# The last spread of O on VectorE instead of GpSimd, with the projection's change of layout ahead of K of pair 31, in a decode-layer kernel

## Chip, cores and metric

The kernel runs on one core of one Trainium2 chip. The metric is the device time of one execution in microseconds (us), and medians over several executions are given. The profile adds a "span", which starts with the first instruction and is in most executions about 1.2 us shorter than the device time. The "granted clock" is the share of TensorE's full clock that the profile shows as granted, 1 or a half in these traces.

## The reference

One decode step of a layer, batch 2, one new token each, D = 512, 32 heads of 128, a KV cache of 8192 positions, then a gated feed-forward of 1376:

```python
q = heads(layernorm(x) @ wq)                                # 32 heads of 128
p = softmax(einsum("bhqd,bhkd->bhqk", q, k_cache) * 128**-0.5)
h = x + merge_heads(einsum("bhqk,bhkd->bhqd", p, v_cache)) @ wo
y = layernorm(h)
gate, up = y @ W_gate, y @ W_up
out = h + ((gate * (gate > 0)) * up) @ W_down
```

The caches are 4 MB for each pair of heads and each of K and V; 281 MB are read in all. That reading sets the time.

## The kernel before

The 64 (batch, head) rows are handled as 32 "pairs" of heads (numbered 0 to 31), two pairs to a round. For each pair the loads bring a 4 MB tile of K and one of V ("K30", "V31" and so on). VectorE computes the scores of three quarters of the positions, of half of them for pair 31 (one multiply, four halving adds, one reduce), TensorE those of the rest (transposes, evacuation by ScalarE, matmuls). ScalarE takes exps, and TensorE multiplies by V ("PV"). After each round the four outputs O are normalised (those of a round while the next one runs) on VectorE and "spread": copied into a sparse matrix `O_l` and a selector `rsel`, from which a small matmul (the "gather") collects the O of all heads but the last two. That spread was GpSimd's:

```python
def o_spread(g):
    pool.wait(t_oc[g], tok("og", g))
    if g >= 1:
        p0, p1 = first(2 * g - 2)[0], first(2 * g - 1)[0]
        pool.run(nc.gpsimd.memset(O_l[:, :, :, p0:min(p1 + NM, 128)], 0.0))
        pool.last()
    for a in range(2):
        p0, off = first(2 * g + a)
        n = min(NM, 128 - p0)
        nc.gpsimd.tensor_copy(out=rsel[:, a, :], in_=rows[:, DR - off:2 * DR - off])
        i = nc.gpsimd.tensor_tensor(out=O_l[:, a, :, p0:p0 + n],
                                    in0=..., in1=..., op=ALU.mult)      # O_cur times mask, cut
    i.then_inc(l2p, 1)
```

TensorE's tail, after the loop over the rounds (P0 = pair 30, P1 = pair 31):

```python
k_part(tail, P0, 1, ...)          # transposes and scores of K30
o_gather(tail)                    # waits for the spread
for r in range(DR): ...           # projection of 30 of the 32 heads by wo: 30 matmuls of 512
k_part(tail, P1, 8, ...)          # transposes and scores of K31, 8 groups
for c in range(DC): ...           # "W": brings the projection into the layout of h
pv(tail, P0, ...)                 # PV30
nc.tensor.wait_ge(a2p, 19)        # all exps of 31
z_sum(tail, Sp[0])                # sums of exps
pv(tail, P1, ...)                 # PV31: first half of V31, then the second
```

Then follow the last two heads' projection, the residual, and the feed-forward: W_up (44 matmuls), W_gate (44), W_down (4 on a piece loaded early, then 40 on three blocks), and the output. The loads of W_up, W_gate and the three W_down blocks are issued in this order after VectorE's multiply of K30 has freed the slot.

The softmax here doesn't subtract the row's maximum and nothing guards it: scores larger than these inputs give would overflow.

## Time and profile before

| | before |
|---|---|
| device time, median | 663.15 us (662.45 to 663.22) |
| span of the profiled execution | 661.4 us |
| HBM read | 281 MB, 425 GB/s over the span |
| share of 16 DMA engines' time with packets | 99.1% |

In all views PE is TensorE, PEld its weight loads, DVE VectorE, ACT ScalarE, POOL GpSimd, and SPq the queue of SyncE, which issues the loads.

DMA is busy to the last slice (9 tenths in 39 of the 40 slices, 6 in the last), so no work in the tail can bring the end far forward: it must wait for the last bytes.

The timeline of GpSimd in the kernel before, around the last two spreads: start in us from the span's start, duration, engine, line, operation, tiles, shape.

```profile
594.08 0.21 POOL L490 COPY rsel<-rows 128x30 bf16<-128x30 bf16 x1
594.24 0.21 POOL L491 TENSOR_TENSOR O_l<-O_cur,mask 128x12 bf16<-128x12 bf16 x1
...
619.01 6.46 POOL L490 COPY rsel<-rows 128x30 bf16<-128x30 bf16 x1
625.42 0.21 POOL L491 TENSOR_TENSOR O_l<-O_cur,mask 128x12 bf16<-128x12 bf16 x1
625.57 3.33 POOL L490 COPY rsel<-rows 128x30 bf16<-128x30 bf16 x1
628.86 0.21 POOL L491 TENSOR_TENSOR O_l<-O_cur,mask 128x10 bf16<-128x10 bf16 x1
```

VectorE in the same stretch of the kernel before:

```profile
618.57 0.16 DVE L470 TENSOR_TENSOR O_cur<-Ob,zi 128x4 bf16<-128x4 f32 x1
618.84 6.56 DVE L516 TENSOR_TENSOR prod<-slot,q_b 128x12288 bf16<-128x12288 bf16 x1
625.43 6.83 DVE L522 TENSOR_TENSOR prod<-prod 128x6144 bf16<-128x6144 bf16 x4
```

The same copy takes 0.21 us in one round and 6.46 us in the last. In the last round VectorE runs its multiply of K30 from 618.84 to 625.40 and its first halving add from 625.43 to 628.84, and the two copies end when these end, at 625.47 and 628.90. The other 28 copies of this form (L490) in the trace ran while VectorE had no instruction, and took 0.207 to 0.209 us each. What in the two VectorE instructions holds up the copies is not shown.

The chain of waits of the kernel before, its end: start, duration, what.

```profile
619.01 6.46 POOL rsel L490
...
625.63 3.28 POOL rsel L490
...
629.75 3.58 PE O L421 x30
633.32 1.03 PE T L349 x4
...
648.30 1.86 PE O L367 x32
...
653.41 1.70 PE S L659 x44
...
655.46 1.66 PE O L659 x44
...
657.55 1.37 PE O L711 x44
```

The spread holds up the projection (L421), that holds up K31's transposes (L349), and so on to PV31 (L367), W_up and W_gate (L659), W_down (L711). No load stands in this last stretch. From the trace's DMA records I took when the last of a transfer's 16 completions landed: V31's second half 647.1, W_up 650.4, W_gate 653.7, last W_down block 656.9. Compute is behind these by only 0.6 to 3 us, so that is what there is to win.

### The profile page before, as it was taken

Reading aid. Unit: us, or ns where it says so; the run is one execution under the profiler, and the core shown is the slowest. Engines: PE = TensorE matmul, PEld = TensorE weight load, DVE = VectorE, ACT = ScalarE, POOL = GpSimd, SP = SyncE. Lnnn points to the kernel's source line nnn. Section 1 sums busy time; section 2 is a strip of 40 time slices with the busy share of each in tenths; the row PEclk is TensorE's granted clock in tenths of the full one; section 3 lists DMA queues with packets and bytes.
Section 4 is the critical chain, followed back from the end, with each engine's and each line's share of the span. In section 5 each row is a group of like instructions: output and inputs, shape, how many; then the busy total and the mean of one; then the engine's idle time right before and its main releaser. Section 6 shows DMA issues by size and latency. Waiting matters only on the chain.

```text
span 661.4 us, 7674 instructions
## 1 busy us (share of the span) xinstructions
PE 333.3 (50%) x3220; PEld 203.4 (31%) x3220; DVE 465.0 (70%) x277; ACT 198.6 (30%) x418; POOL 34.0 (5%) x126
## 2 busy tenths in 40 slices
PE   2652354444555444645535364554536444454487
PEld 2431322223333122423313243232324322232254
DVE  1775576788767678776767877676886767687681
ACT  0531331233332223333223333322323322232360
POOL 2000000000000000000000000000000000000510
PEclk9995565556555656565555565655565565555787
DMA  9999999999999999999999999999999999999996
GB/s 381 430 415 428 444 421 432 436 422 442 426 432 438 425 432 432 428 440 426 432 434 424 440 427 430 438 428 434 432 427 434 430 432 432 430 437 430 426 424 257
DMA packets 10787, 281.23 MB, mean 425 GB/s; under 512 B 1202, under 2 KB 1556, under 8 KB 1940
## 3 DMA queue, kind: packets, MB, share of 16 engines
q1 hardware_dynamic: 10760, 281.06, 99.1%
q8 instruction: 6, 0.10, 0.1%
q14 instruction: 9, 0.07, 0.0%
q10 hardware_dynamic: 12, 0.00, 0.0%
HBM read 281.05 MB, written 0.00 MB: 425 GB/s over the span
## 4 chain that ended last, share of the span: by engine, by line
DMA 76%; DVE 16%; PE 4%; POOL 2%; ACT 1%; issue 0%; SPq 0%; DVEq 0%
DMA slot<-in_A_k_cache_dram 76%; DVE prod L516 15%; POOL rsel L490 1%; PE O L367 1%; DVE prod L522 1%; ACT kT L547 1%; PE O L421 1%; PE T L349 0%; PE Ob L377 0%; PE W L428 0%; PE S L659 0%; PE O L659 0%; PE S L337 0%; PE O L711 0%; DVE scores L527 0%
## 5 line engine op out<-in xcount | busy, mean ns | idle before, releaser
L516 DVE TENSOR_TENSOR prod<-slot,q_b 128x12288 bf16<-128x12288 bf16 (+1 forms) x32 | 207.7, 6491 | 152.5 <-DMA slot<-in_A_k_cache_dram 150.7
L522 DVE TENSOR_TENSOR prod<-prod 128x6144 bf16<-128x6144 bf16 (+4 forms) x128 | 210.3, 1643 | 4.4
L367 PE MATMUL O<-slot,e 128*16 128x512 bf16 x1024 | 118.5, 616 | 185.3 <-ACT e L454 129.7
L547 ACT ACTIVATE kT<-T 128x1024 bf16<-128x1024 bf16 x132 | 131.0, 1022 | 189.3 <-PE T L349 186.0
L349 PE MATMUL T<-ident_f,slot 128*128 128x128 f32 x528 | 121.8, 390 | 51.6 <-POOLq L534 51.6
L349 PEld LDWEIGHTS T<-ident_f,slot 128*128 128x128 f32 x528 | 87.9, 200 | 66.8 <-issue 66.7
L367 PEld LDWEIGHTS O<-slot,e 128*16 128x16 bf16 x1024 | 25.9, 112 | 251.8 <-ACT e L454 157.6
L454 ACT ACTIVATE e<-scores 64x96 bf16<-64x96 f32 (+1 forms) x64 | 19.4, 303 | 209.9 <-DVE scores L527 209.4
L337 PE MATMUL S<-q2c,kT 128*128 128x4 bf16 x1056 | 49.8, 169 | 39.0 <-ACT kT L547 38.7
L337 PEld LDWEIGHTS S<-q2c,kT 128*128 128x128 bf16 x1056 | 42.7, 106 | 67.3 <-ACT kT L547 65.3
L377 PE MATMUL Ob<-sel,os_sb 128*128 128x4 f32 x136 | 30.2, 345 | 24.9 <-ACT os_sb L562 24.2
L377 PEld LDWEIGHTS Ob<-sel,os_sb 128*128 128x128 f32 x136 | 28.7, 312 | 26.8 <-ACT os_sb L562 25.6
L527 DVE TENSOR_REDUCE scores<-prod 128x96 f32<-128x768 bf16 (+1 forms) x32 | 30.2, 945 | 1.1
L499 POOL COPY q2c<-q 128x8 bf16<-128x8 bf16 x32 | 9.1, 284 | 235.1 <-DMA slot<-in_A_v_cache_dram 221.2
L485 POOL MEMSET O_l<- 128x40 bf16 (+1 forms) x14 | 1.9, 136 | 325.9 <-DVE O_cur L470 325.9
L490 POOL COPY rsel<-rows 128x30 bf16<-128x30 bf16 x30 | 15.6, 520 | 34.4 <-DVE O_cur L470 33.5
L454 ACT ACTIVATE e<-S 64x32 bf16<-64x32 f32 (+1 forms) x64 | 13.0, 203 | 14.4 <-PE S L337 14.0
L454 ACT ACTIVATION_READ_ACCUMULATOR e<-S 64x1 f32 x64 | 12.8, 201 | 0.7
L454 ACT ACTIVATION_READ_ACCUMULATOR e<-scores 64x1 f32 x64 | 11.8, 184 | 0.0
L383 PEld LDWEIGHTS Ob<-zs,ones_f 128*128 128x128 f32 x30 | 7.0, 292 | 12.8 <-issue 12.8
L562 ACT ACTIVATE os_sb<-O 128x512 f32<-128x512 f32 x16 | 9.6, 597 | 3.2 <-PE O L367 2.8
L298 ACT ACTIVATE q_b<-O 128x512 bf16<-128x512 f32 x8 | 4.3, 595 | 17.4 <-PE O L293 17.4
(90 smaller groups left out, 85.6 us busy)
## 6 DMA issues: line engine op xcount, KB each, us to landing
slot<-in_A_k_cache_dram SPq DMA_DIRECT2D x32, 4096.0 KB, 32.3
slot<-in_A_v_cache_dram SPq DMA_DIRECT2D x31, 4096.0 KB, 30.6
slot<-in_A_wq_dram SPq DMA_DIRECT2D x1, 4096.0 KB, 12.3
slot<-in_A_v_cache_dram SPq DMA_DIRECT2D x2, 2048.0 KB, 28.0
X<-in_A_wo_dram SPq DMA_DIRECT2D x1, 3840.0 KB, 46.5
slot<-in_B_W_up_dram SPq DMA_DIRECT2D x1, 1376.0 KB, 25.0
slot<-in_B_W_gate_dram SPq DMA_DIRECT2D x1, 1376.0 KB, 27.9
slot<-in_B_W_down_dram SPq DMA_DIRECT2D x2, 512.0 KB, 29.1
```

Source lines behind the costliest of these rows:

```text
L337: i = nc.tensor.matmul(Sp[p % 2][:, 2 * jj:2 * jj + 4], lhsT=kv_[:, k, r, :], rhs=q2c[p % 2][:, r, :], start=(r == 0), stop=(r == 1))
L349: i = nc.tensor.transpose(Tp[g % 2][:, k * 128:(k + 1) * 128], k_t[:, j:j + 2, :].rearrange("p j d -> p (j d)").bitcast(F32), ident_f[:])
L367: i = nc.tensor.matmul(Op[0][c:c + 16, :], lhsT=e_t[q][:, j // VJ, :], rhs=v_t[:, j:j + VJ, :].rearrange("p j d -> p (j d)"), start=(q == ...
L377: i = nc.tensor.matmul(Ob[:, 0:4], lhsT=os_sb[:, jj * Dh:(jj + 1) * Dh], rhs=sel[:, 4 * jj:4 * jj + 4], start=(jj == 0), stop=(jj == VJ - 1))
L454: i = nc.scalar.activation(out=e_t[q][h, j0 // VJ:j1 // VJ, 8 * q:8 * q + 8].rearrange("p g (j a) -> p g j a", a=2)[:, :, :, a], in_=src(h ...
L490: nc.gpsimd.tensor_copy(out=rsel[:, a, :], in_=rows[:, DR - off:2 * DR - off])
L499: nc.gpsimd.tensor_copy(out=q2c[p % 2][:], in_=q2[:, p]).then_inc(g2p, 1)
L516: t_dm[p] = dve.run(nc.vector.tensor_tensor(out=prod[:, 0:jd, :], in0=k_t[:, 0:jd, :], in1=qv, op=ALU.mult))
L522: dve.run(nc.vector.tensor_tensor(out=prod[:, 0:jd, 0:half], in0=prod[:, 0:jd, 0:half], in1=prod[:, 0:jd, half:w], op=ALU.add))
L527: t_s[p] = dve.run(nc.vector.tensor_reduce(out=sc[:, 0:jd], in_=prod[:, 0:jd, 0:w], axis=AX.X, op=ALU.add))
L547: to_pe(nc.scalar.activation(out=kT[gg % 2][:], in_=Tp[gg % 2][:].bitcast(BF16), func=ACT.Copy))
L562: to_pe(nc.scalar.activation(out=os_sb[:], in_=Op[0][:], func=ACT.Copy))
```

## The change

Its intent: the last spread goes to VectorE, ahead of K30's multiply, so that no copy of it runs beside that multiply; the projection's result is brought into h's layout before K31 is transposed; the exps of pair 30 stand between the fourth and fifth evacuation of K31, and the sums of exps between the halves of PV31. The core of the diff:

```diff
 # TensorE's tail
-k_part(tail, P1, 8, ...)
 nc.tensor.wait_ge(a2p, 8)
 for c in range(DC): ...                                # W
-pv(tail, P0, ((j30, J, ...), (0, j30, ((a2p, 17),))))
-nc.tensor.wait_ge(a2p, 19)
-z_sum(tail, Sp[0])
-pv(tail, P1, ((j31, J, ((sem_vl[0], 16),)), (0, j31, ((sem_vl[1], 16),))))
+k_part(tail, P1, (9, 10, 11, 12, 14, 15, 16, 17), ...)
+pv(tail, P0, ((j30, J, ...), (0, j30, ((a2p, 13),))))
+pv(tail, P1, ((j31, J, ((sem_vl[0], 16), (a2p, 18))), (0, j31, ((a2p, 19), (sem_vl[1], 16)))),
+   lambda: z_sum(tail, Sp[0]))
...
 # VectorE and GpSimd
 if p == P0:
     o_norm(g - 1, t_ob_loop)
+    o_spread(g - 1, dve)          # memset, two copies, two multiplies
...
-if p % 2 == 0 and p >= 2:
-    o_spread(g - 1)
+if p % 2 == 0 and 2 <= p < P0:
+    o_spread(g - 1, pool)
...
 # ScalarE, pair 31
-evacs()
+evacs(0, NG)
 exp_dve(P0, j30)
+evacs(NG)
```

More of the change, by code (lines that the diff above doesn't have):

```diff
@@ L324, in program, with k_part @@
                 body = Tokens(pe.count)
-                def k_part(T, p, a0, k_wait):
+                def k_part(T, p, ev, k_wait):
                     s, ng = (2 * p) % 4, split(p)[0]
@@ L331, in score @@
                     def score(g):
-                        wait(a2p, a0 + 1 + g)
+                        wait(a2p, ev[g])
                         kv_ = kT[g % 2][:].rearrange("p (k n r) -> p k r n", n=128, r=2)
@@ L345, in k_part @@
                         if g >= 2:
-                            wait(a2p, a0 + 1 + g - 2)
+                            wait(a2p, ev[g - 2])
                         for k in range(GT // 2):
@@ L355, in k_part, with pv @@
                     score(ng - 1)
-                def pv(T, p, parts):
+                def pv(T, p, parts, between=None):
                     s = (2 * p + 1) % 4
@@ L362, in pv @@
                     for j0, j1, waits in parts:
+                        if between and n:
+                            nc.tensor.wait_ge(*waits[0])
+                            between()
                         for sem, val in waits:
@@ L386, in o_gather @@
                 def o_gather(T):
-                    nc.tensor.wait_ge(l2p, 1)
                     for a in range(2):
@@ L396, in program @@
                     jd = split(0)[1]
-                    k_part(body, 0, 0, ((g2p, 1), (v2p, 1)))
+                    k_part(body, 0, (1, 2, 3, 4), ((g2p, 1), (v2p, 1)))
                     collect(body, 6)
                     pv(body, 0, ((jd, J, ((v2p, 2), (a2p, 5))), (0, jd, ((a2p, 7),))))
-                    k_part(body, 1, 7, ((g2p, 2), (v2p, 3)))
+                    k_part(body, 1, (8, 9, 10, 11), ((g2p, 2), (v2p, 3)))
+                    nc.tensor.wait_ge(l2p, 1)
                     o_gather(body)
@@ L415, in program @@
                 t_ob_loop = (pe.sem, tail.at["ob"])
-                k_part(tail, P0, 1, ((slot_sem[0], 256), (g2p, 1)))
+                k_part(tail, P0, (2, 3, 4, 5), ((slot_sem[0], 256), (g2p, 1)))
+                nc.tensor.wait_ge(l2p, 1)
                 o_gather(tail)
@@ L424, in program @@
                 tail.mark("op", i)
-                k_part(tail, P1, 8, ((slot_sem[2], 256), (g2p, 2)))
                 nc.tensor.wait_ge(a2p, 8)
@@ L430, in program @@
                         start=False, stop=False, skip_group_check=True)
-                pv(tail, P0, ((j30, J, ((slot_sem[1], 256), (a2p, 6))), (0, j30, ((a2p, 17),))))
-                nc.tensor.wait_ge(a2p, 19)
-                z_sum(tail, Sp[0])
-                pv(tail, P1, ((j31, J, ((sem_vl[0], 16),)), (0, j31, ((sem_vl[1], 16),))))
+                k_part(tail, P1, (9, 10, 11, 12, 14, 15, 16, 17), ((slot_sem[2], 256), (g2p, 2)))
+                pv(tail, P0, ((j30, J, ((slot_sem[1], 256), (a2p, 6))), (0, j30, ((a2p, 13),))))
+                pv(tail, P1, ((j31, J, ((sem_vl[0], 16), (a2p, 18))), (0, j31, ((a2p, 19), (sem_vl[1], 16)))),
+                   lambda: z_sum(tail, Sp[0]))
                 def tok(key, g):
@@ L479, in o_norm, with o_spread @@
                     t_oc[g] = dve.run(o_scale())
-                def o_spread(g):
-                    pool.wait(t_oc[g], tok("og", g))
+                def o_spread(g, prog):
+                    e = prog.eng
+                    prog.wait(t_oc[g], tok("og", g))
                     if g >= 1:
                         p0, p1 = first(2 * g - 2)[0], first(2 * g - 1)[0]
-                        pool.run(nc.gpsimd.memset(O_l[:, :, :, p0:min(p1 + NM, 128)], 0.0))
-                        pool.last()
+                        prog.run(e.memset(O_l[:, :, :, p0:min(p1 + NM, 128)], 0.0))
+                        prog.last()
                     for a in range(2):
@@ L489, in o_spread @@
                         n = min(NM, 128 - p0)
-                        nc.gpsimd.tensor_copy(out=rsel[:, a, :], in_=rows[:, DR - off:2 * DR - off])
-                        i = nc.gpsimd.tensor_tensor(
+                        e.tensor_copy(out=rsel[:, a, :], in_=rows[:, DR - off:2 * DR - off])
+                        i = e.tensor_tensor(
                             out=O_l[:, a, :, p0:p0 + n],
@@ L534, in program, with evacs @@
                             nc.gpsimd.sem_inc(v2p, 1)
-                    if p % 2 == 0 and p >= 2:
-                        o_spread(g - 1)
+                    if p % 2 == 0 and 2 <= p < P0:
+                        o_spread(g - 1, pool)
                     if p < P1:
                         q_copy(p + 1)
-                    def evacs():
-                        for gg in range(ng):
+                    def evacs(g0=0, g1=ng):
+                        for gg in range(g0, g1):
                             act.wait(tokp("pt", p, gg))
```

## The prediction

The forecast's sum comes to a gain of 1.1 to 1.6 us.

> What bounds the kernel now. The DMA queue. The page shows DMA at 9 tenths in 39 of 40 slices, 281 MB read, 425 GB/s over the span; the chain of waits is 76% DMA. Landing times in the trace (last of a transfer's 16 completions, us from the span's start): V29 608.2, K30 617.9, K31 627.6, V30 637.4, V31 first half 642.2, second half 647.1, W_up 650.5, W_gate 653.8, last W_down block 656.9; the windows view agrees (full rate to 654, nothing after 657). All are issued by 627.7 and stand in a backlog (25 to 30 us to landing), so no compute change in the tail moves them.
>
> The chain of waits shows where the change aims: O_cur 618.6, then on POOL a spread of 10.3 us: two 128x30 copies of 6.46 and 3.28 us that took 0.21 us in the round before. They end when the VectorE multiply (625.4) and the first halving add (628.8) end. [...] PE waits 6.2 us for it (629.1), projects 30 matmuls (3.58 us), transposes K31 only from 633.25, ACT evacuates 8 times 0.98 us to 642.2, PV30 ends 647.9, PV31 650.2.
>
> What changes. VectorE does the spread before K30's multiply: memset, two copies, two multiplies, about 0.17 us each by its neighbours (0.16 to 0.18), estimate 0.9 us. K30's multiply starts near 619.8, not 618.84; DVE ends its last reduce near 644.2, not 643.27. PE has the gather at 623.2, the projection to 627.7, W to about 630.4; K31 (landed 627.6) is transposed from 630.4, not 633.25. The exps of 30 stand after four evacuations, near 636, so PV30 follows k_part directly (about 640.7 to 644.2) and the first half of PV31 at once. That makes compute 3 us or more earlier before V31's last half.
>
> How much counts. PV31's second half cannot start before 647.1 (landing). It takes 0.93 us at full granted clock, 1.9 at half: ends 648.1 to 649.0, not 650.2. The following sums to the first W_up matmul take 3.2 us as now (650.19 to 653.41): 651.3 to 652.2. W_up work 1.7 plus transposes 0.35 ends 653.4 to 654.2; W_gate landed 653.8; gate ends 655.5 to 655.9; W_down starts 0.43 later, 656.0 to 656.4; its last block landed 656.9; end near 657.3 to 657.8 against 658.92. The rest, 2.5 us, is unchanged. Gain 1.1 to 1.6 us of the 10 us that the spread gives back: the DMA backlog eats the rest. Floor: last landing 656.9 plus 8 matmuls, so at most 1.7 us can be won.
>
> Predicted: 661.8 us, 661.0 to 662.9 (before: 662.45 to 663.22). Faster by over 2%: 0.01; within 2%: 0.98; slower: 0.01.
>
> What would show it. (1) VectorE: five small instructions before K30's multiply, 0.8 to 1.1 us in all; no POOL instruction over 0.5 us after 600. (2) Gather right after K30's scores, near 623. (3) K31's transposes start 630 to 631. (4) PE idle before PV31's second half until V31's landing near 647: a DMA wait new in the chain. (5) Landings within 0.3 us of before. (6) W_up's first matmul 651.3 to 652.2. (7) Last W_down matmul 657.3 to 657.8.
>
> What would make it wrong. The granted PE clock falls differently (full only in 617 to 624, 634 to 644 and 648 to 655 now): half clock in the end costs up to 1 us. VectorE's last exps, near 645, could come later than V31's landing if the spread costs 3 us. Landings that shift by 1 us between executions would outweigh the gain. If W_gate or W_down waits were not binding at 653.8 and 656.9, the gain could reach 2 us.

## More of the kernel before

The page of the kernel before: the DMA line gives the busy tenths of the DMA engines in 40 equal slices of the span, and part 4 is the chain of waits that ended last.

```profile
DMA  9999999999999999999999999999999999999996
...
q1 hardware_dynamic: 10760, 281.06, 99.1%
q8 instruction: 6, 0.10, 0.1%
q14 instruction: 9, 0.07, 0.0%
...
DMA 76%; DVE 16%; PE 4%; POOL 2%; ACT 1%; issue 0%; SPq 0%; DVEq 0%
```

## The result, and the profile after

The changed kernel takes 662.24 us (661.97 to 662.91, four runs) against 663.15 us. The ratio is 0.999, 95% interval 0.9973 to 1.0007. Ratios here are the mean time of one kernel's runs over that of the other's of the same rounds, so not quite the ratio of the medians. The time lies in the predicted range; the gain of 0.9 us by the medians (0.5 us between the profiled spans) is below the 1.1 to 1.6 us that were forecast. The predicted range, 661.0 to 662.9, overlaps the runs of the kernel before (662.45 to 663.22), so a time inside it says little by itself.

The timeline of VectorE in the changed kernel, around the spread:

```profile
619.56 0.16 DVE L473 TENSOR_TENSOR O_cur<-Ob,zi 128x4 bf16<-128x4 f32 x1
619.81 0.10 DVE L489 MEMSET O_l<- 128x44 bf16 x1
619.94 0.18 DVE L494 COPY rsel<-rows 128x30 bf16<-128x30 bf16 x1
620.03 0.17 DVE L495 TENSOR_TENSOR O_l<-O_cur,mask 128x12 bf16<-128x12 bf16 x1
620.11 0.17 DVE L494 COPY rsel<-rows 128x30 bf16<-128x30 bf16 x1
620.18 0.17 DVE L495 TENSOR_TENSOR O_l<-O_cur,mask 128x10 bf16<-128x10 bf16 x1
620.26 6.55 DVE L521 TENSOR_TENSOR prod<-slot,q_b 128x12288 bf16<-128x12288 bf16 x1
```

Ten microseconds of spread have become half of one (619.81 to the multiply at 620.26). The last four start 0.07 to 0.09 us apart though each takes 0.17 to 0.18 us: they overlap.

The timeline of TensorE in the changed kernel: projection, K31's first transposes, PV30 with the first half of PV31, its second half, W_up, W_gate, and the three W_down groups. In brackets stands the idle time before, with what ended it.

```profile
626.35 3.17 PE L425 MATMUL O<-X,O_all 128*2 128x512 bf16 x30 [1.07 <-ACT O_all L580]
...
632.10 1.69 PE L349 MATMUL T<-ident_f,slot 128*128 128x128 f32 x8
...
643.37 4.06 PE L370 MATMUL O<-slot,e 128*16 128x512 bf16 x48
...
647.68 1.04 PE L370 MATMUL O<-slot,e 128*16 128x512 bf16 x16
...
652.00 1.74 PE L665 MATMUL S<-d_b,slot 128*128 128x2 bf16 x44 [0.26 <-DVE d_b L645]
...
654.01 1.72 PE L665 MATMUL O<-d_b,slot 128*128 128x2 bf16 x44
...
656.17 0.28 PE L717 MATMUL O<-wd_last,hd 96*2 96x128 bf16 x4 [0.30 <-DVE ve L708]
656.23 0.64 PE L717 MATMUL O<-slot,hd 128*2 128x128 bf16 x16
657.38 1.02 PE L717 MATMUL O<-slot,hd 128*2 128x128 bf16 x24 [0.51 <-DMA slot<-in_B_W_down_dram]
```

Up to 656.17 everything is 1.4 us ahead of the kernel before (W_up 652.00 for 653.41, W_down 656.17 for 657.55). Then W_down stops twice for its blocks, and it ends at 658.4, only 0.5 us ahead of the 658.9 of the kernel before. The chain of waits of the changed kernel ends accordingly; the tail of the kernel before had no such line:

```profile
628.16 29.18 DMA slot<-in_B_W_down_dram
657.34 0.04 issue
657.38 0.60 PE O L717 x12
657.98 0.04 issue
658.02 0.41 PE O L717 x7
```

So most of the 1.4 us was taken back by a load that came late. The question is why it did: the last landing moved from 656.9 to 658.0, while V31's (647.3) and W_gate's (653.9) had moved by 0.2 us only. Looking at the 16 completions of each W_down block one by one, 15 are where they were and one is a microsecond behind them. Packets in the trace carry no engine number, but in the sequence below each packet starts within 0.011 us of the end of the one before it, and I take it for the sequence of the late engine (start in us, bytes, duration in us; an inference from the times). An instruction fetch is a packet on a queue that the page calls "instruction"; the nine of 8 KB in this span took 0.31 to 0.33 us each.

```
654.176  4096 B  0.164
654.336  4096 B  0.169
654.501  8192 B  0.326   instruction fetch (queue 14)
654.816  4096 B  0.500
655.308  4096 B  0.476
655.781  4096 B  0.159
...
657.525     4 B  0.009   completion of the last W_down block (on its semaphore at 657.98)
```

An 8 KB instruction fetch of some engine stands in the middle of W_down, and with the two slowed packets after it costs this DMA engine 0.96 us (by the starts, against 0.16 us for a packet: 0.32 + 0.33 + 0.31). Of the 256 packets of 4096 B that start after 650 us in this trace, these two took 0.50 and 0.48 us; the median is 0.16. In the kernel before, the fetch with this place in the sequence starts at 658.4, after all weights have landed.

### The profile page after: what moved, and what is told of

Its sections match the earlier page's. It is cut to its first block, busy times and chain, and to the rows that moved or that the text cites. A ratio compares the mean times of both kernels' runs of the same rounds, so it can differ in the third digit from the quotient of the medians.

```text
span 660.9 us, 7674 instructions
## 1 busy us (share of the span) xinstructions
PE 338.3 (51%) x3220; PEld 208.2 (31%) x3220; DVE 465.6 (70%) x282; ACT 198.9 (30%) x418; POOL 22.5 (3%) x121
## 4 chain that ended last, share of the span: by engine, by line
DMA 80%; DVE 17%; PE 1%; SPq 1%; issue 0%; ACT 0%; DVEq 0%
DMA slot<-in_A_k_cache_dram 76%; DVE prod L521 16%; DMA slot<-in_B_W_down_dram 4%; DVE prod L527 1%; PE O L370 0%; PE Ob L380 0%; PE O L717 0%; DVE scores L532 0%; SPq L167 0%; SPq L609 0%; ACT e L457 0%; ACT os_sb L567 0%; SPq L173 0%; SPq L176 0%; SPq L613 0%
## 5 line engine op out<-in xcount | busy, mean ns | idle before, releaser
L349 PE MATMUL T<-ident_f,slot 128*128 128x128 f32 x528 | 126.7, 401 | 51.4 <-POOLq L539 51.4
L349 PEld LDWEIGHTS T<-ident_f,slot 128*128 128x128 f32 x528 | 91.6, 206 | 65.7 <-issue 65.7
L503 POOL COPY q2c<-q 128x8 bf16<-128x8 bf16 x32 | 7.6, 238 | 235.3 <-DMA slot<-in_A_v_cache_dram 221.3
L386 PE MATMUL Ob<-zs,ones_f 128*128 128x8 f32 x30 | 8.6, 361 | 0.0
```

Of the source, the lines that this page charges most:

```text
L349: i = nc.tensor.transpose(Tp[g % 2][:, k * 128:(k + 1) * 128], k_t[:, j:j + 2, :].rearrange("p j d -> p (j d)").bitcast(F32), ident_f[:])
L386: T.mark("z", nc.tensor.matmul(bank[:, ZC:ZC + 8], lhsT=ones_f[:], rhs=zs[:], start=True, stop=True))
L503: nc.gpsimd.tensor_copy(out=q2c[p % 2][:], in_=q2[:, p]).then_inc(g2p, 1)
```

## The experiments

Theory A: the fetch is VectorE's. Its program grew from 321 to 325 instructions (five operations more, one separate wait fewer), and in both traces 319 of them had begun when the fetch started, at 658.4 and at 654.5: with more instructions ahead of that place, and compute earlier as well, VectorE reaches it earlier. By this theory its fetch now falls among the W_down packets of a DMA engine that is among the last anyway. Rivals: A', a 16 KB fetch (queue 8) that I took for TensorE's, which moved from 656.8 to 655.3; B, the weight loads are issued 1.4 us later (626.84 for 625.43), since VectorE's multiply comes later; C, chance between executions.

For all kernels the records give the following (us from the start of each trace's own span; "W_down minus W_up" is the last landing of the last W_down block minus that of W_up; with VectorE's +112 it is 6.41, for 6.46 in the kernel before, though the whole backlog runs late and the last landing is at 657.9):

```
kernel                       8 KB fetch after 600   W_down last   W_down minus W_up
before                       658.4                  656.9         6.46
changed                      654.5                  658.0         7.42
changed, again               654.6                  657.9         7.44
changed, VectorE +112        none                   657.9         6.41
changed, TensorE +144        656.0                  658.0         7.44
changed, both                none                   657.7         6.43
changed, VectorE -8          661.9                  657.1         6.46
before, VectorE +8           656.6                  657.3         6.71
spread alone                 654.9                  657.8         7.40
order alone                  661.9                  656.8         6.44
before, VectorE -8           none                   656.9         6.47
changed, VectorE -8, again   660.8                  656.6         6.45
spread alone, VectorE -8     661.7                  656.8         6.42
one reordering, VectorE -8   660.9                  656.8         6.45
```

### The changed kernel again

No edit.

> The changed kernel once more, with its trace. If the late W_down landing is a property of this program (theories A, B), one of the 16 completions of each W_down block comes again about 1 us after the others, the last near 658.0 us, and an 8 KB instruction fetch starts near 654.5. If it was chance (theory C), the last landing is back near 656.9 and the span near 659.9.

Measured: 662.26 us, ratio to before 0.9993 (0.998 to 1.0007), span 660.8. The fetch started at 654.6, and one completion of the last block came 1.09 us after the other 15, at 657.9. It belongs to the program; C falls.

### 112 instructions more on VectorE, 144 more on TensorE, and both

The edits add waits on a semaphore that has long been reached (by my count two of them make one instruction):

```diff
+if 8 <= p < 16:
+    for _ in range(28):
+        nc.vector.wait_ge(sem_x, 16)      # 8 x 14 instructions, VectorE idle there
 dve.wait((slot_sem[s], 16 * (g + 1)), t_q_b)
```
```diff
+for _ in range(288):
+    nc.tensor.wait_ge(sem_x, 16)          # 144 instructions, ahead of the loop
 body = Tokens(pe.count)
```

The clauses that are cut from the first two of the expectations below said how far VectorE's and TensorE's last fetches would move; the figures in them were not shown by a trace. What the runs ask is whether W_down's landing changes when the one fetch or the other moves.

> 112 extra VectorE waits that are long met, in eight tiles of the loop where VectorE idles for K, shift its instruction stream [...]. Theory A (the 8 KB fetch is VectorE's, and it delays W_down on one DMA engine): no 8 KB fetch between 645 and 657, last W_down landing near 656.9 to 657.0, last projection matmul near 657.3, span 659.8 to 660.1, about 1 us faster than the changed kernel. Theory B (weights issued 1.4 us later) and theory A' (TensorE's 16 KB fetch): landing and span as in the changed kernel, 660.9.

Measured: 663.23 us, ratio 1.0007 (0.9994 to 1.0021), span 661.4. The fetch of 654.5 is gone, so it is VectorE's, and W_down came 6.41 us after W_up. But the expected time did not come: the last completion of each load was late already, that of W_down at 657.9. The padding bought one more fetch in the loop (two, at 265.5 and 423.1, for one at 383.4), and the trace shows what the second did. How far the last of 16 completions of a tile lay behind the next to last: 0.42 us for the tile that landed at 413.9, 1.43 us for the one at 424.6, 1.10 us for K31 at 628.6, 1.04 us for W_down at 657.9. In this backlog most of the microsecond that was lost at 423 was still lost 230 us later. I had expected the padding to be free; it only moved the cost.

> 144 extra TensorE waits that are long met, in the setup, shift TensorE's instruction stream [...]. Theory A': last W_down landing near 656.9, span near 659.9. Theory A and B: the 8 KB fetch stays near 654.5 and the landing near 658.0, span 660.9.

Measured: 662.26 us, ratio 0.9989 (0.9976 to 1.0003), span 661.5. The 16 KB fetches moved with TensorE's padding, so they are TensorE's: the last two stood at 654.5 and 662.8, in the changed kernel at 650.8 and 655.3. W_down was as late as before the padding (7.44). The 8 KB fetch came at 656.0, 1.5 us later than in the changed kernel, as did VectorE's work here, but still among the packets of W_down. A' falls.

> Both shifts. Theory A or A': last landing near 656.9, span 659.8 to 660.1, 0.4% faster than before. Theory B: 660.9 as the changed kernel.

Measured: 663.73 us, ratio 1.0009 (0.9995 to 1.0022), span of the profiled execution 660.7. As with VectorE's padding alone: no late fetch, 6.43, but a late backlog (after a fetch at 422.9 the last completion was 1.11 us behind at 424.4, and still 1.00 us at 657.7). The expected gain was missed for the same reason.

### 8 instructions fewer on VectorE

This makes VectorE's program shorter and not longer, and was expected to add no fetch. In the setup, six waits are dropped that another wait implies, a memset goes to GpSimd, and a reduction becomes three small adds there:

```diff
 for m in range(NP // 4):
     if m >= 2:
         dve.wait(t_mm[m - 2])
-    dve.last()
+    else:
+        dve.last()
...
-dve.run(nc.vector.memset(q2[:], 0.0))                  # to GpSimd
-dve.run(nc.vector.tensor_reduce(out=sel2[:], ...))     # to GpSimd, as three adds
```

> The changed kernel with 8 VectorE instructions fewer in the setup (six waits that were already implied, a memset and a reduction that GpSimd takes over), and nothing else. Unlike the padded kernel it adds no instruction fetch anywhere. Theory A: VectorE never comes to the point where it fetched at 654.5, no 8 KB fetch between 645 and 658, the last W_down landing comes 6.4 to 6.5 us after W_up's (as before the change; 7.4 in the changed kernel), near 656.9, the last W_down matmul ends near 657.5, span 659.7 to 660.1, 1 us below the changed kernel. Theory B (weights issued later): 7.4 us after W_up's and 660.9 still. Theory C (chance): anything.

Measured: 662.25 us, ratio 0.9978 (0.9964 to 0.9992), correct. No 8 KB fetch before 661.9, the last landing at 657.1, 6.46 after W_up's: A holds, and B falls, since the loads were issued as late as in the changed kernel (626.86). The span was missed in the profiled execution, 661.2; the five executions lie between 659.7 and 661.2. There W_up's first matmul came only at 653.39: the granted clock of TensorE was half through the projection and all of K31's part (0.50 from 624.0 to 644.0), and PV started at 644.05 and not 643.37.

```profile
644.05 4.77 PE L374 MATMUL O<-slot,e 128*16 128x512 bf16 x48
...
653.39 1.56 PE L669 MATMUL S<-d_b,slot 128*128 128x2 bf16 x44 [0.26 <-DVE d_b L649]
```

So in this execution compute, and not the last landing, set the end. A second trace on another chip:

> The changed kernel with 8 fewer, once more on this chip, for a second trace. Last landing near 656.9 again. Where TensorE's granted clock is full in PV31, W_up's first matmul comes at 652.0 and the span is 659.7 to 660.2; where it stays half from 624 on as in the first trace, 653.4 and 661.2.

Measured: 661.43 us, ratio 0.9979 (0.9965 to 0.9992), span 660.0. TensorE's timeline in this execution, to be read beside that of the changed kernel above:

```profile
652.10 1.70 PE L669 MATMUL S<-d_b,slot 128*128 128x2 bf16 x44 [0.26 <-DVE d_b L649]
...
656.23 0.28 PE L721 MATMUL O<-wd_last,hd 96*2 96x128 bf16 x4 [0.30 <-DVE ve L712]
656.29 1.28 PE L721 MATMUL O<-slot,hd 128*2 128x128 bf16 x40
```

W_up and the first W_down matmuls start within 0.1 us of those in the changed kernel, and the 40 matmuls on the three blocks now run without a stop, to 657.6 and not 658.4. TensorE's own fetch stood at 655.5 here, beside 655.3 in the changed kernel, and did no harm: A' falls a second time.

The windows of these two executions give the spread that is left; the columns are the stretch, its length, busy us (and instructions) of TensorE, its weight loads, VectorE, ScalarE, GpSimd, then the granted clock, the DMA share and GB/s. First the execution with the span of 661.2, with K31's part and PV:

```profile
632.40:644.00 11.60, 10.07 (x98) 8.11 (x97) 11.26 (x9) 8.72 (x12) 0.00 (x0) 0.50 0.97 414
644.00:650.20 6.20, 6.11 (x71) 2.16 (x68) 0.95 (x3) 1.60 (x9) 0.00 (x0) 0.66 0.99 418
```

and the one with the span of 660.0:

```profile
632.00:643.00 11.00, 9.21 (x95) 7.27 (x96) 10.69 (x7) 8.72 (x12) 0.00 (x0) 0.54 0.98 417
643.00:648.80 5.80, 5.80 (x74) 2.14 (x71) 1.46 (x4) 1.57 (x8) 0.00 (x0) 0.70 1.00 423
```

From K31's first transpose to the end of PV31 the first execution took 17.6 us (632.52 to 650.11) and the second 16.8 us (632.06 to 648.82): 0.8 us longer in the execution whose granted clock was 0.50 and 0.66 in these two windows, where the other had 0.54 and 0.70. The rest of the difference of 1.2 us does not arise in this stretch: the first execution was 0.46 us behind before it, and so were its landings (V31's second half at 647.27 and 646.81). In the clock records of the traces of the kernel before and of the changed kernel the changes are 3.41 us apart or multiples of it: full from 617.11 to 623.93 and from 647.82 to 654.65 before, from 628.98 to 632.39 and from 646.04 to 652.87 after.

### Controls on the kernel before

> Control: the kernel before with the same 8 VectorE instructions fewer. Theory A: its 8 KB fetch at 658.4 came after the last weight had landed, so nothing is won: span 661.4 within its usual spread, ratio 0.999 to 1.001, last landing 6.4 to 6.5 us after W_up's. If the setup itself got faster by what was taken out, it shows here as a gain of the same 1 us as in the changed kernel.

Measured: 663.11 us, ratio 0.9994 (0.9981 to 1.0008), span 661.9, W_down minus W_up 6.47. The 8 instructions fewer win nothing where the fetch came after the weights, as expected: their worth in the changed kernel is the fetch, not a faster setup.

The same kernel with 8 instructions more (16 waits of the kind above, in one tile):

> The kernel before with 8 more VectorE waits that are long met, in one idle stretch of the loop; no other change. Theory A: its 8 KB fetch moves from 658.4 to about 654.5, among the W_down blocks, and the last landing moves from 656.9 to about 657.9, 7.4 us after W_up's; the time stays, within 0.3 us, since compute comes to W_down only at 657.5 and to the last block at 658.7. Theory B: the landing stays at 656.9, as the weights are issued where they were.

Measured: 663.60 us, ratio 1.0004 (0.999 to 1.0018), span 662.7. The fetch moved forward, but only to 656.6, and the landing to 657.3 (6.71 after W_up's). The direction is A's, but the shift against W_up is 0.25 us where 0.95 us was expected: the fetch met only the end of W_down. The time is the same, since compute reached the W_down blocks at 658.96, later than that. The traces also tell where the fetch stands in VectorE's program. The number of VectorE's recorded instructions (waits included) that had begun when it started is 319 in six traces (before, changed, changed again, TensorE +144, spread alone, order alone) and 321 in this one; the programs with 8 fewer have 317 or 313 in all. So the fetch belongs to a nearly fixed place in the program, and its time is the time at which VectorE gets there: the 319th began at 654.18 in the changed kernel and at 657.51 in the kernel before. The 8 KB fetches of 660.8 to 661.9 in the programs with 317 start about 3 us after VectorE's last instruction; whose they are is not shown.

### The parts of the change

> The kernel before with only the spread moved to VectorE; order of TensorE and of the exps as before. Projection from about 626, K31's transposes from about 630, PV31 ends 648.3 to 649.2, W_up's first matmul 651.5 to 652.5; the same 8 KB fetch near 654.5 and the last landing near 658.0: span 660.7 to 661.1. If the reordering is what gives the gain, W_up's first matmul comes at 653 or later.

Measured: 662.10 us, ratio 0.9984 (0.9971 to 0.9998), span 660.7. Projection at 626.10, K31's transposes at 629.61, W_up's first matmul at 652.41, the late fetch at 654.9. By time, the spread alone gives what the whole change gives. PV31 ended at about 649.1 here, 0.4 us after the whole change; its first half still stood behind the sums of exps.

> The changed kernel with the spread back on GpSimd. The spread again takes 10 us, the gather comes at 629, K31's transposes only after W, near 636; PV31 ends 650 to 652, span 661.2 to 662.8, same as the kernel before or slower. VectorE's stream is as long as before, so no 8 KB fetch before 657 and the last landing is near 656.9.

Measured: 665.69 us, ratio 1.0029 (1.0013 to 1.0044), span 664.9: slower, by more than expected. GpSimd's timeline in this kernel shows the old spread back:

```profile
619.79 6.46 POOL L494 COPY rsel<-rows 128x30 bf16<-128x30 bf16 x1
...
626.36 3.34 POOL L494 COPY rsel<-rows 128x30 bf16<-128x30 bf16 x1
```

The projection starts at 630.53, W at 634.79, and K31's transposes at 636.68, for 633.25 before the change. The last landing was on time, 656.8; compute was what ended last. The reordering needs the fast spread.

> Only the spread on VectorE, with 8 fewer, old order. No 8 KB fetch before 658, last landing near 656.9, W_up's first matmul near 652.4, last W_down matmul near 657.9, span 660.0 to 660.4, as good as the whole change with 8 fewer: then the two reorderings are worth nothing here.

Measured: 661.77 us, ratio 0.9975 (0.9962 to 0.9989), spans 659.7 to 661.2. No late fetch, landing at 656.8. In the profiled execution W_up's first matmul came at 653.06 and the span was 661.0, so both were missed there (652.4 and 660.0 to 660.4 were expected). By its ratio it equals the whole change with 8 fewer.

> The same with one part of the reordering: the sums of exps of 31 stand between the halves of PV31, and W stays behind K31's part. The first half of PV31 starts near 644.4 and not 645.7, the second at V31's landing 647.2; W_up's first matmul 651.2 to 652.2, bound by the last landing 656.9: span 659.6 to 660.0, the fastest of all, 0.995 to 0.997 of before.

This one adds to the spread alone, with 8 fewer, only the sums of exps between the halves of PV31. Measured: 661.60 us, ratio 0.9979 (0.9965 to 0.9993), spans 660.2 to 661.2. The second half of PV31 did start with V31's landing, at 647.12, and W_up at 652.27; but it is not faster than the other two, and no execution reached the expected span. The three kernels with 8 fewer cannot be told apart by time. Each of them beats the kernel before, and the ratio of each lies below those of the changed kernel (0.999 and 0.9993), though the intervals overlap.

## Why the prediction was right or wrong

- **What bounds it: right.** The DMA queue; compute could win only what it was behind the landings.
- **The slow copies and their cure: right.** The spread fell from about 10 us to about half of one (10.28 us from 618.79 to 629.07 before, 0.54 from 619.81 to 620.35 after), and no GpSimd instruction runs after 609. VectorE's five instructions delay K30's multiply, measured from the end of O_cur, by 0.43 us more than before (0.54 for 0.11), where the prediction's estimate was 0.9: they were counted one after the other, but overlap.
- **Gather at 623 and K31's transposes at 630 to 631: wrong by 2 and 1.5 us, without effect.** They came at 625.0 and 632.1. In this execution TensorE's granted clock was half in K30's part (0.50 from 618.5 to 625.0), where it had been full from 617.1 to 623.9 in the trace before.
- **TensorE idle until V31 lands: wrong, without much effect.** K31's part took 11.3 us at a granted clock of 0.51 (9.35 us before, at 0.95), so PV30 and the first half of PV31 reached to 647.4; V31 had landed at 647.3. The second half started at 647.68 and not 647.1.
- **W_up's first matmul 651.3 to 652.2, W_down 656.0 to 656.4: right.** 652.00 and 656.17. The gain up to here is 1.4 us.
- **"Landings within 0.3 us of before": this is the step that failed**, and with it "its last block landed 656.9; end near 657.3 to 657.8". In the prediction's words, "no compute change in the tail moves them". The change moved one: the last W_down block landed at 658.0 and W_down ended at 658.4. The term of the sum that was mis-sized is the last landing, by 1.1 us in the two profiled executions (0.96 us of it after W_up).
- **The cause, shown:** VectorE's instruction fetch. It comes and goes with VectorE's instruction count (gone with 112 more or 8 fewer), not with TensorE's; in the four traces with it between 654.5 and 656.0 the last W_down landing comes 7.40 to 7.44 us after W_up's, in the nine with it absent or after 658 it comes 6.41 to 6.47 us after. The spread alone, with the fetch, and the changed kernel with 8 fewer, without it, ran on one chip in the same rounds (7.40 and 6.46). With the fetch out of the way and nothing else changed in the tail, the change is worth what was forecast: ratios 0.9978 and 0.9979, which is 1.4 to 1.5 us of 663 (0.5 to 2.4 us by the intervals), against a forecast of 1.3 us in the middle.
- **Not shown:** why the two packets after the fetch are slow, and why VectorE's fetch fell on a DMA engine that was among the last in each of those four traces. Not every 8 KB fetch shows in the last landing: in the changed kernel the one at 592.9 left the last completion of the next tile 0.07 us behind the next to last, where it had been 0.08. Nor do the times alone prove that taking the fetch out makes the kernel faster: the intervals of 0.9993 (0.998 to 1.0007) and 0.9978 (0.9964 to 0.9992) overlap. The landings, not the times, carry the proof.

## What to carry to other kernels

In the changed kernel's tail the last landing of the 16 completions was the floor (W_down's last matmuls waited for it until 657.98), and an instruction fetch of 0.33 us, with the two slowed packets after it, put it off by 0.96 us: look in the DMA records for packets that are not yours, and see what stands behind them. Here four instructions more on VectorE, together with compute that came 1.4 us earlier, put a fetch among the packets of the last load, and eight fewer brought its landing back by a microsecond (from 658.0 to 657.1 and 656.6 in two traces); padding did not help where it bought another fetch, since the lag lasted to the end (1.43 us at 424.6, 1.04 us at 657.9). And when an instruction on GpSimd takes thirty times its usual time (6.46 us for 0.21 us here), see which VectorE instruction ends with it before reordering anything: here the move to VectorE alone gave all of the gain (ratio 0.9984), and the reordering alone lost time (1.0029).
